# A decode attention and gated MLP kernel: gate scaling folded into the PSUM accumulation, the last V group loaded in quarters, and the small edits beside them

## The chip, the cores and the metric

The kernel runs on one core of a Trainium2 chip. The metric is the device time of one execution in microseconds (us). In the profiles PE is the matmul engine, PEld its weight loads, DVE, ACT and POOL the other compute engines, and SP the engine that issues the loads; the granted clock is the share of its full clock that PE was given. A load has landed when its last byte is in place. Ratios compare runs taken in the same rounds on the same chip.

## The reference

```python
x = A_x                                   # [1, 1, 448], bfloat16
g = sigmoid((x * gate_w).sum(-1))
a = attention(x, k_cache, v_cache, wq, wo) # 16 query heads, 8 KV heads,
                                          # 65536 keys of 256, softmax, then @ wo
gate, up = x @ W_gate, x @ W_up           # [448, 1792]
b = (relu(gate) * up) @ W_down            # [1792, 448]
return g * a + (1 - g) * b
```

The K and V caches are 537 MB. Everything else is small: wq and wo 3.67 MB each, the three MLP ("FFN") weights 1.6 MB each.

## The kernel before

A planner in Python simulates the engines, decides the order of all instructions, and emits them with semaphore waits. All loads are issued in order by one queue (SP). K comes in groups of 4096 rows (2 MB) into a ring of five slots: three for groups that PE transposes and multiplies ("T"), two for groups that DVE reduces ("D"). V comes in groups of 2 MB into a ring of three slots. After the last K group, the FFN weights are loaded over the K ring, while V of the last two heads still has to come.

The parts, with cuts marked by `...`:

```python
# a weight load; extra_w are the K ring slots that the FFN weights overwrite
def emit_wdma(key, dst, src, extra_w=()):
    ...
    return A("sp", lambda e: e.dma_start(dst, src), w=[key] + list(extra_w), dma=(s_w[i], 16), ...)

# rows of a [448, n] weight: 3 x 128 on 128 partitions, then 64 on 64 partitions
def wparts(name, dst, src):
    parts = [(name + "a", dst[:, 0:KFULL, :], src[0:KFULL * 128, :].rearrange("(k p) n -> p k n", p=128))]
    if KREM:
        parts.append((name + "b", dst[0:KREM, KFULL, :], src[KFULL * 128:D, :]))
    return parts

# P @ V: two V rows side by side, so a head's result lies on 4 partitions as two halves
def emit_pv(g, grp, slot, j0, j1, first, last): ...   # 16 matmuls of 128x4 by 128x512 a group

# after the last V group of a head: copy, transpose, scale by 1/denominator, multiply by wo
def emit_oc(g): ...   # ACT copy O_ps -> o_raw, 4x512 float32
def emit_ft(g): ...   # 4 transposes
def emit_on(g): ...   # 4 scalings (half x head)
def emit_am(g): ...   # 8 matmuls into A_ps (half x chunk x head)

def emit_final():
    # DVE: res = b * (1 - g);  res_bf = A_ps * g + res;  then SP stores
    ...
```

In the planner's bookkeeping `w` is a write that must wait for the last writer and all readers of a key. `w2` is a write by one of several writers, which need not wait for each other. A DMA that is the last writer of a key is waited for until it has landed.

## Time and profile before

| | before |
|---|---|
| median of 16 runs (lowest, highest) | 1373.2 us (1371.2, 1379.2) |
| span of the profiled run | 1369.5 us |
| read from HBM | 549.03 MB |
| busy share: PE, DVE, ACT, DMA queue | 82%, 80%, 30%, 96.5% |

The DMA rate of the page, in 40 slices of 34 us. It stays between 381 and 430 GB/s in most slices, and the DMA queue is busy for 96.5% of the span: the loads bound this kernel. Slice 35 (1164 to 1198 us) drops to 273.

```profile
GB/s 341 398 396 423 428 392 416 414 401 404 419 412 425 406 419 396 395 430 416 426 357 421 413 414 429 381 430 398 424 407 362 428 423 411 273 404 428 428 428 260
```

The last 140 us before the last landing carry nothing but V and run at 428 GB/s, one group of 2 MB in 4.90 us. No stretch of 100 us in this trace is above 430 (the highest is 429). I take 428 as an estimate of the full rate, from these 140 us. On that estimate time can only come from stretches in which the DMA engines move less.

What SP waited for (total us, times, longest us). The first three lines are the ring: a load waits for its slot. These waits come to 1196.5 us, and yet the DMA queue was busy for 96.5% of the span, so most of them cost nothing. The last two are different: one FFN weight load waits until the one before it has landed.

```profile
SPq L137 <- PE O_ps L575: 524.0, 93, 17.1
SPq L137 <- PE KTp L430: 419.2, 59, 31.5
SPq L137 <- DVE S_T L460: 253.3, 35, 20.3
...
SPq L363 <- DMA kring<-in_B_W_gate_dram: 17.0, 2, 14.4
SPq L363 <- DMA kring<-in_B_W_up_dram: 9.0, 2, 6.5
```

The same stretch by windows of 10 us. The columns after the length are busy us of PE, PE weight load, DVE, ACT and POOL with their instructions, then granted clock, DMA share and GB/s. Two windows move 110 and 160 GB/s at a DMA share of 0.34 and 0.47.

```profile
1170.00:1180.00 10.00, 6.83 (x31) 2.59 (x32) 6.39 (x36) 0.20 (x1) 0.37 (x1) 1.00 0.99 420
1180.00:1190.00 10.00, 8.39 (x65) 4.25 (x63) 0.33 (x2) 5.94 (x18) 0.46 (x1) 1.00 0.34 110
1190.00:1200.00 10.00, 3.89 (x57) 3.45 (x55) 0.00 (x0) 0.00 (x0) 0.00 (x0) 0.53 0.47 160
1200.00:1210.00 10.00, 2.33 (x33) 2.04 (x32) 0.41 (x3) 0.00 (x0) 0.00 (x0) 0.50 1.06 409
1210.00:1220.00 10.00, 9.70 (x45) 3.74 (x46) 1.06 (x2) 0.00 (x0) 0.00 (x0) 0.78 1.00 428
```

The end (timeline: start, duration, engine, line, operation). The last V group has landed at 1358.6; 10.8 us follow in which no load moves data.

```profile
1358.64 3.62 PE L575 MATMUL O_ps<-vraw,PTd 128*4 128x512 bf16 x16 [1.23 <-DMA vraw<-in_A_v_cache_dram]
1362.30 0.58 ACT L582 COPY o_raw<-O_ps 4x512 f32<-4x512 f32 x1 [77.09 <-PE O_ps L575]
...
1362.93 0.41 PE L590 MATMUL M_ps<-identf,o_raw 4*128 4x4 f32 x4 [0.67 <-ACT o_raw L582]
1363.42 0.72 ACT L602 ACTIVATE oT<-M_ps,rden 128x2 bf16<-128x2 f32 x4 [0.55 <-PE M_ps L590]
...
1364.29 2.84 PE L617 MATMUL A_ps<-wo_sb,oT 128*1 128x448 bf16 x8 [0.95 <-ACT oT L602]
...
1367.25 0.67 DVE L652 SCALAR_TENSOR_TENSOR res_bf<-A_ps,gsc,junk 1x448 bf16<-1x448 f32 x1 [148.38 <-PE A_ps L617]
1367.95 0.31 SPq L655 DMA_DIRECT2D out_dram<-res_bf  x1
```

### The profile page before, as it was taken

What the parts mean: (1) busy time and instruction counts of PE and PEld (TensorE: products, weight loads), DVE (VectorE), ACT (ScalarE), POOL (GpSimd) and SP (SyncE); (2) the same over time, 40 slices, a digit from 0 to 9 for tenths busy, and PEclk for the clock granted to TensorE, in tenths of its full rate; (3) what the DMA queues carried; (4) which work ended last, traced back from release to release, by engine and by line L of the source; (5) the groups of instructions that cost most, each with busy time, mean ns of one, the idle gap of its engine ahead of it and who ended that gap; (6) DMA issues with size and microseconds to landing.
All of it is one profiled execution on the core that took longest, in us unless ns stands there. A gap on an engine that the chain in (4) does not pass through costs nothing.

```text
span 1369.5 us, 20913 instructions
## 1 busy us (share of the span) xinstructions
PE 1117.2 (82%) x6256; PEld 614.2 (45%) x6338; DVE 1094.9 (80%) x6218; ACT 410.3 (30%) x818; POOL 13.7 (1%) x29
## 2 busy tenths in 40 slices
PE   4899899987999669987699966999659896667777
PEld 3577657542664226642265422764227542232222
DVE  1999989999989999899999699989997999300000
ACT  2466556421552105530054400552007420100000
POOL 1000000000000000000000000000000000000000
PEclk9999999998999899998999999999989999879999
DMA  8999999999999999999989999999999999699996
GB/s 341 398 396 423 428 392 416 414 401 404 419 412 425 406 419 396 395 430 416 426 357 421 413 414 429 381 430 398 424 407 362 428 423 411 273 404 428 428 428 260
DMA packets 45300, 550.38 MB, mean 402 GB/s; under 512 B 5185, under 2 KB 11074, under 8 KB 11970
## 3 DMA queue, kind: packets, MB, share of 16 engines
q1 hardware_dynamic: 45186, 549.05, 96.5%
q8 instruction: 49, 0.80, 0.2%
q14 instruction: 65, 0.53, 0.1%
HBM read 549.03 MB, written 0.00 MB: 401 GB/s over the span
## 4 chain that ended last, share of the span: by engine, by line
PE 40%; DMA 38%; DVE 19%; issue 1%; ACT 1%; SPq 1%; ACTq 0%; DVEq 0%
DMA vraw<-in_A_v_cache_dram 23%; DVE junk L460 18%; PE KTp L430 14%; PE S_ps L444 13%; PE O_ps L575 12%; DMA kring<-in_A_k_cache_dram 11%; DMA kring<-in_B_W_gate_dram 1%; DMA vraw<-in_A_wq_dram 1%; DMA kring<-in_B_W_up_dram 1%; PE M_ps L387 1%; DVE MXW L474 1%; DVE S_T L460 1%; SPq L371 0%; ACT kts L435 0%; ACT P_sb L505 0%
## 5 line engine op out<-in xcount | busy, mean ns | idle before, releaser
L460 DVE CUSTOM_DVE_ANT_0 junk<-kring,qb 128x256 bf16<-128x256 bf16 x3072 | 1064.8, 419 | 0.6 <-ACT qb L424 0.2
L435 ACT COPY kts<-KTp 128x512 f32<-128x512 f32 x640 | 347.8, 592 | 382.1 <-PE KTp L430 381.6
L575 PE MATMUL O_ps<-vraw,PT_sb 128*4 128x512 bf16 x1280 | 308.6, 397 | 102.3 <-DMA vraw<-in_A_v_cache_dram 102.1
L430 PE MATMUL KTp<-identf,kring 128*128 128x128 f32 x2560 | 345.2, 277 | 32.2 <-DMA kring<-in_A_k_cache_dram 32.2
L430 PEld LDWEIGHTS KTp<-identf,kring 128*128 128x128 f32 x2560 | 305.3, 143 | 115.2 <-DMA kring<-in_A_k_cache_dram 37.9
L444 PE MATMUL S_ps<-kts,zq 128*128 128x512 bf16 x1198 | 336.8, 390 | 9.4 <-issue 2.6
L575 PE MATMUL O_ps<-vraw,PTd 128*4 128x512 bf16 x768 | 191.4, 407 | 72.7 <-DMA vraw<-in_A_v_cache_dram 72.5
L460 DVE DVE_READ_ACCUMULATOR2_ANT S_T<- 128x1 f32 x3072 | 247.6, 81 | 0.0
L575 PEld LDWEIGHTS O_ps<-vraw,PT_sb 128*4 128x4 bf16 x1280 | 109.2, 90 | 292.9 <-DMA vraw<-in_A_v_cache_dram 129.2
L444 PEld LDWEIGHTS S_ps<-kts,zq 128*128 128x128 bf16 x1280 | 109.6, 98 | 97.3 <-ACT kts L435 40.4
L575 PEld LDWEIGHTS O_ps<-vraw,PTd 128*4 128x4 bf16 x768 | 65.0, 89 | 195.6 <-DMA vraw<-in_A_v_cache_dram 91.2
L582 ACT COPY o_raw<-O_ps 4x512 f32<-4x512 f32 x8 | 4.6, 575 | 413.7 <-PE O_ps L575 413.7
L652 DVE SCALAR_TENSOR_TENSOR res_bf<-A_ps,gsc,junk 1x448 bf16<-1x448 f32 x1 | 0.7, 672 | 148.4 <-PE A_ps L617 148.4
L474 DVE TENSOR_REDUCE MXW<-S_sb 64x1 f32<-64x512 f32 (+1 forms) x32 | 21.7, 678 | 45.8 <-ACT S_sb L450 45.1
L498 ACT ACTIVATE nbias<-negm 128x2 f32<-128x2 f32 x8 | 1.7, 209 | 103.8 <-DVE negm L496 103.8
L387 PE MATMUL M_ps<-xT,vraw 128*128 128x1 bf16 (+1 forms) x128 | 9.2, 174 | 17.4 <-DMA vraw<-in_A_wq_dram 17.4
L505 ACT ACTIVATE P_sb<-S_sb,nbias 64x512 bf16<-64x512 f32 (+1 forms) x32 | 22.9, 717 | 0.6
L402 DVE CAST zq<-M_ps 128x32 bf16<-128x32 f32 x1 | 0.3, 295 | 26.9 <-PE M_ps L394 26.9
L387 PEld LDWEIGHTS M_ps<-xT,vraw 128*128 128x128 bf16 (+1 forms) x128 | 8.3, 106 | 18.2 <-issue 17.3
L617 PE MATMUL A_ps<-wo_sb,oT 128*1 128x448 bf16 x64 | 14.6, 374 | 1.2 <-ACT oT L602 1.2
L545 DVE TENSOR_REDUCE den<-den 128x2 f32<-128x6 f32 x8 | 1.3, 158 | 17.8 <-POOL den L538 17.7
L450 ACT COPY S_sb<-S_ps 128x512 f32<-128x512 f32 x16 | 9.4, 588 | 16.4 <-PE S_ps L444 16.4
(47 smaller groups left out, 103.7 us busy)
## 6 DMA issues: line engine op xcount, KB each, us to landing
kring<-in_A_k_cache_dram SPq DMA_DIRECT2D x128, 2048.0 KB, 12.4
vraw<-in_A_v_cache_dram SPq DMA_DIRECT2D x128, 2048.0 KB, 14.7
wo_sb<-in_A_wo_dram SPq DMA_DIRECT2D x1, 3584.0 KB, 46.1
vraw<-in_A_wq_dram SPq DMA_DIRECT2D x1, 3072.0 KB, 12.1
kring<-in_B_W_down_dram SPq DMA_DIRECT2D x1, 1568.0 KB, 7.2
kring<-in_B_W_gate_dram SPq DMA_DIRECT2D x1, 1344.0 KB, 14.8
kring<-in_B_W_up_dram SPq DMA_DIRECT2D x1, 1344.0 KB, 6.9
vraw<-in_A_wq_dram SPq DMA_DIRECT2D x1, 512.0 KB, 13.6
```

The source lines that it names most:

```text
L387: A("pe", (lambda hc=hc, kt=kt, kk=kk, wv=wv: lambda e: e.matmul(M_ps[:, MC_Q + hc:MC_Q + hc + 1], lhsT=wv, rhs=xT[0:kk, kt:kt + 1], start ...
L430: A("pe", (lambda j=j, jj=jj: lambda e: e.transpose(out=KTp[bank][:, jj * 128:(jj + 1) * 128], in_=tring[:, slot, j, :].bitcast(F32), iden ...
L435: A("act", lambda e: e.copy(out=kts[:, kbuf, :].bitcast(F32), in_=KTp[bank][:, :]), pr=PQ(B_K + bank), w=[("kts", kbuf)], tag=f"ev b{bank} ...
L444: A("pe", (lambda r=r, par=par, rhs=rhs, first=first, last=last: lambda e: e.matmul(S_ps[sphys][:, :], lhsT=zq[:, g, par, 63 - r:191 - r], ...
L450: A("act", lambda e: e.copy(out=S_sb[:, pb, b, :], in_=S_ps[sphys][:, :]), pr=PQ(B_S + sphys), w=[("ssb", pb, b)], tag=f"scopy g{g} b{b}")
L460: A("dve", (lambda j=j, hh=hh, col=col, ji=ji: lambda e: e.tensor_tensor_reduce(out=junk[:, ji, :], in0=dring[:, slot, j, :], in1=qb[:, g, ...
L474: A("dve", (lambda hh=hh, p0=p0: lambda e: e.tensor_reduce(out=MXW[p0:p0 + ns, pb, 2 + 2 * b + hh:3 + 2 * b + hh], in_=S_sb[p0:p0 + ns, pb ...
L498: A("act", lambda e: e.activation(out=nbias[:, pb, :], in_=negm[:, pb, :], func=ACT.Copy, scale=SCALE), r=[("negm", pb)], w=[("nbias", pb) ...
L505: A("act", lambda e: e.activation(out=P_sb[p0:p0 + ns, pb, b, :], in_=S_sb[p0:p0 + ns, pb, b, :], func=ACT.Exp, bias=nbias[p0:p0 + ns, pb, ...
L575: A("pe", (lambda lhs=lhs, rhs=rhs, f_=f_, l_=l_: lambda e: e.matmul(O_ps[qd:qd + 4, 0:2 * DH], lhsT=lhs, rhs=rhs, start=f_, stop=l_))(), ...
L582: A("act", lambda e: e.copy(out=o_raw[qd:qd + 4, :], in_=O_ps[qd:qd + 4, 0:2 * DH]), pr=PQ(B_O, qd, qd + 4), w=[("oraw", pb)], tag=f"oc g{g}")
L617: A("pe", (lambda oc_=oc_, hc=hc, first=first, last=last: lambda e: e.matmul(A_ps[0:1, 0:D], lhsT=oT[:, pb, oc_:oc_ + 1], rhs=wo_sb[:, hc, :],
```

## The change

Its intent, by its title: fold the gate (g and 1 - g) into the accumulation of the output in PSUM, so that the DVE combination at the end goes away, and load the last V group in four parts, so that PE can begin before all of it has landed. The diff holds four more edits that the title does not name. Cut to its core:

```diff
 # 1. claims of the FFN loads
-    return A("sp", ..., w=[key] + list(extra_w), dma=(s_w[i], 16), ...)
+    return A("sp", ..., w=[key], w2=list(extra_w), dma=(s_w[i], 16), ...)
 # 2. start: wq is issued before the tiny x and gate_w loads
-        push_w(small, 4096)
-        push_w(wparts("wq", wq_sb, A_wq), ..., done=wq_done)
+        push_w(wparts("wq", wq_sb, A_wq), ...)
+        push_w(small, 4096, done=wq_done)
 # 3. gate: [g, 1-g] broadcast once by POOL; g into the scaling of a head's result ...
+            A("pool", lambda e: e.partition_all_reduce(gb[:], gz[:], 128, ...add), ...)
+            A("dve", ... rdg[:, g, :] = rden[:, g, :] * gb[:, 0:1])
 #    ... and 1-g into h; the down-projection accumulates into A_ps as well
-                    O_ps[64:65, 0:D], lhsT=hT[:, ft:ft + 1], rhs=wd_sb[:, ft, :], ...
+                    A_ps[0:1, 0:D], lhsT=hT[:, ft:ft + 1], rhs=wd_sb[:, ft, :], start=False, stop=False))(),
-            # DVE: b * (1-g), then A_ps * g + that; SP stores
+            A("act", lambda e: e.activation(out=res_bf[:], in_=A_ps[0:1, 0:D], func=ACT.Copy), ...)  # ACT stores
 # 4. the two halves of a head's result are summed while transposing: 4 float32 matmuls with a
 #    selection matrix instead of 4 transposes; 2 scalings instead of 4; 4 wo matmuls instead of 8
+                        M_ps[:, col:col + 2], lhsT=o_raw[qd:qd + 4, part * DH + c * 128:...],
+                        rhs=identf[qd:qd + 4, qd + 2 * part:...], start=(part == 0), stop=(part == 1)
 # 5. every V group is handed to PE in four quarters (planner), score matmuls may come between
+                    for part in range(VSUB):
+                        arrived[c].append((g, grp, slot, part))
 # 6. the last V group of the last head is also loaded in four quarters
+            split = (c == "V" and g == HKV - 1 and grp == NG - 1)
```

The instruction streams, compared engine by engine, show that the order of the loads is otherwise the same. The waits on the weight loads' semaphores are gone.

More of the change, by code (lines that the diff above doesn't have):

```diff
@@ L208, in bass_gated_mix__gqa_block_cached__glu_gated_reglu__decode_kernel @@
     F = B_W_gate.shape[1]
-    assert DH == 256 and HQ == 2 * HKV and F % 128 == 0
+    assert DH == 256 and HQ == 2 * HKV and F % 128 == 0 and HKV >= 2
     NC2 = 2
@@ L296, in bass_gated_mix__gqa_block_cached__glu_gated_reglu__decode_kernel @@
         hT = sb("hT", [128, FT], BF16)
-        b_sb = sb("b_sb", [1, D], F32)
         gsc = sb("gsc", [1, 4], F32)
@@ L308, in bass_gated_mix__gqa_block_cached__glu_gated_reglu__decode_kernel @@
         o_raw = sb("o_raw", [64, 2 * DH], F32)
-        oT = sb("oT", [128, 2, 8], BF16)
-        res = junk[0:1, :, :].rearrange("p a d -> p (a d)").bitcast(F32)[:, 0:D]
+        oT = sb("oT", [128, 2, 4], BF16)
+        gz = sb("gz", [128, 2], F32)
+        gb = sb("gb", [128, 2], F32)
+        rdg = sb("rdg", [128, HKV, 2], F32)
         res_bf = sb("res_bf", [1, D], BF16)
@@ L352, in emit_consts @@
             A("pool", lambda e: e.memset(warm[:], 0.0), w=["warm"])
+            A("pool", lambda e: e.memset(gz[:], 0.0), w=["gzz", "gz0"])
             A("pool", lambda e: e.partition_all_reduce(warm[:, 2:4], warm[:, 0:2], 128, bass.bass_isa.ReduceOp.max),
@@ L362, in emit_wdma, with emit_group_dma @@
             wsem_i[0] += 1
-            return A("sp", lambda e: e.dma_start(dst, src), w=[key] + list(extra_w), dma=(s_w[i], 16), tag=f"wdma {key}")
-        def emit_group_dma(cls, g, grp, slot):
+            return A("sp", lambda e: e.dma_start(dst, src), w=[key], w2=list(extra_w), dma=(s_w[i], 16), tag=f"wdma {key}")
+        VSUB = 4 if J % 8 == 0 else 2
+        JP = J // VSUB
+        s_vsub = [sem(f"s_vsub{i}") for i in range(VSUB)]
+        vsub_cnt = [0] * VSUB
+        def emit_group_dma(cls, g, grp, slot, part=None):
             src_t = A_v_cache if cls == "V" else A_k_cache
@@ L369, in emit_group_dma @@
             dst = ring[:, slot, :, :]
-            ring_cnt[cls][slot] += 1
-            A("sp", lambda e: e.dma_start(dst, src), w=[(cls, slot)],
-              after=(wq_readers if cls == "V" and ring_cnt[cls][slot] == 1 else ()),
-              dma=(ring_sems[cls][slot], 16 * ring_cnt[cls][slot]), tag=f"dma{cls} g{g} grp{grp}")
+            if part is None:
+                ring_cnt[cls][slot] += 1
+                first_use = ring_cnt[cls][slot] == 1
+                keys = [(cls, slot)] if cls != "V" else [("V", slot, p_) for p_ in range(VSUB)]
+                dsem = (ring_sems[cls][slot], 16 * ring_cnt[cls][slot])
+            else:
+                src = src[:, part * JP:(part + 1) * JP, :]
+                dst = dst[:, part * JP:(part + 1) * JP, :]
+                vsub_cnt[part] += 1
+                first_use = False
+                keys = [("V", slot, part)]
+                dsem = (s_vsub[part], 16 * vsub_cnt[part])
+            A("sp", lambda e: e.dma_start(dst, src), w=keys,
+              after=(wq_readers if cls == "V" and first_use else ()),
+              dma=dsem, tag=f"dma{cls} g{g} grp{grp}")
         x_keys = ["xT0"] + (["xT1"] if KREM else [])
@@ L409, in emit_zq @@
               r=[("gsc", 0), ("gsc", 2)], w=[("gsc", 3)])
+            A("dve", lambda e: e.tensor_copy(out=gz[0:1, :], in_=gsc[0:1, 2:4]), r=[("gsc", 2), ("gsc", 3)], w=["gz0"], tag="gz")
+            A("pool", lambda e: e.partition_all_reduce(gb[:], gz[:], 128, bass.bass_isa.ReduceOp.add),
+              r=["gz0", "gzz"], w=["gb"], tag="gb")
         def emit_qb_mm(g, bank):
@@ L548, in emit_rcp @@
               tag=f"rcp g{g}")
+            A("dve", lambda e: e.tensor_scalar(out=rdg[:, g, :], in0=rden[:, g, :], scalar1=gb[:, 0:1], scalar2=None,
+                                               op0=AluOpType.mult), r=[("rden", g), "gb"], w=[("rdg", g)], tag=f"rdg g{g}")
         def slot_of(g, ti, j):
@@ L576, in emit_pv @@
                     O_ps[qd:qd + 4, 0:2 * DH], lhsT=lhs, rhs=rhs, start=f_, stop=l_))(),
-                  r=[("V", slot)] + rk, pw=PQ(B_O, qd, qd + 4), tag=f"pv g{g} grp{grp}")
+                  r=[("V", slot, j // JP)] + rk, pw=PQ(B_O, qd, qd + 4), tag=f"pv g{g} grp{grp}")
         def emit_oc(g):
@@ L587, in emit_ft @@
             qd = 32 * pb
-            for i in range(4):
-                col = MC_OT + pb * 16 + i * 4
-                A("pe", (lambda i=i, col=col: lambda e: e.transpose(
-                    out=M_ps[:, col:col + 4], in_=o_raw[qd:qd + 4, i * 128:(i + 1) * 128],
-                    identity=identf[qd:qd + 4, qd:qd + 4]))(),
-                  r=[("oraw", pb), "identf"], pw=PQ(B_M), tag=f"ft g{g}")
+            for c in range(NC2):
+                col = MC_OT + pb * 4 + c * 2
+                for part in range(2):
+                    A("pe", (lambda c=c, col=col, part=part: lambda e: e.matmul(
+                        M_ps[:, col:col + 2], lhsT=o_raw[qd:qd + 4, part * DH + c * 128:part * DH + (c + 1) * 128],
+                        rhs=identf[qd:qd + 4, qd + 2 * part:qd + 2 * part + 2], start=(part == 0), stop=(part == 1)))(),
+                      r=[("oraw", pb), "identf"], pw=PQ(B_M), tag=f"ft g{g}")
         def emit_on(g):
             pb = g % 2
-            for part in range(2):
-                for hh in range(2):
-                    c0 = MC_OT + pb * 16 + part * 8 + 2 * part + hh
-                    src = M_ps[:, c0:c0 + 8].rearrange("p (c k) -> p c k", k=4)[:, :, 0]
-                    dst = oT[:, pb, part * 4:part * 4 + 4].rearrange("p (c h) -> p h c", h=2)[:, hh, :]
-                    A("act", (lambda src=src, dst=dst, hh=hh: lambda e: e.activation(
-                        out=dst, in_=src, func=ACT.Copy, scale=rden[:, g, hh:hh + 1]))(),
-                      r=[("rden", g)], pr=PQ(B_M), w=[("oT", pb, part, hh)], tag=f"on g{g}")
+            for hh in range(2):
+                src = M_ps[:, MC_OT + pb * 4:MC_OT + pb * 4 + 4].rearrange("p (c h) -> p h c", h=2)[:, hh, :]
+                dst = oT[:, pb, :].rearrange("p (c h) -> p h c", h=2)[:, hh, :]
+                A("act", (lambda src=src, dst=dst, hh=hh: lambda e: e.activation(
+                    out=dst, in_=src, func=ACT.Copy, scale=rdg[:, g, hh:hh + 1]))(),
+                  r=[("rdg", g)], pr=PQ(B_M), w=[("oT", pb, hh)], tag=f"on g{g}")
         def emit_am(g):
@@ L608, in emit_am @@
             n = 0
-            for part in range(2):
-                for c in range(NC2):
-                    for hh in range(2):
-                        n += 1
-                        first = (g == 0 and n == 1)
-                        last = (g == HKV - 1 and n == 4 * NC2)
-                        hc = (2 * g + hh) * NC2 + c
-                        oc_ = part * 4 + c * 2 + hh
-                        A("pe", (lambda oc_=oc_, hc=hc, first=first, last=last: lambda e: e.matmul(
-                            A_ps[0:1, 0:D], lhsT=oT[:, pb, oc_:oc_ + 1], rhs=wo_sb[:, hc, :],
-                            start=first, stop=last))(),
-                          r=[("oT", pb, a_, b_) for a_ in range(2) for b_ in range(2)] + ["wo"], pw=PQ(B_A, 0, 1),
-                          tag=f"am g{g}")
+            for c in range(NC2):
+                for hh in range(2):
+                    n += 1
+                    first = (g == 0 and n == 1)
+                    last = (g == HKV - 1 and n == 2 * NC2)
+                    hc = (2 * g + hh) * NC2 + c
+                    A("pe", (lambda c=c, hh=hh, hc=hc, first=first, last=last: lambda e: e.matmul(
+                        A_ps[0:1, 0:D], lhsT=oT[:, pb, 2 * c + hh:2 * c + hh + 1], rhs=wo_sb[:, hc, :],
+                        start=first, stop=last))(),
+                      r=[("oT", pb, 0), ("oT", pb, 1), "wo"], pw=PQ(B_A, 0, 1), tag=f"am g{g}")
         def emit_gu(which):
@@ L636, in emit_h @@
             A("dve", lambda e: e.tensor_copy(out=u_bf[:], in_=M_ps[:, MC_U:MC_U + FT]), pr=PQ(B_M), w=["u_bf"], tag="h")
-            A("dve", lambda e: e.tensor_tensor(out=hT[:], in0=g_bf[:], in1=u_bf[:], op=AluOpType.mult),
-              r=["g_bf", "u_bf"], w=["hT"], tag="h")
+            A("dve", lambda e: e.scalar_tensor_tensor(out=hT[:], in0=g_bf[:], scalar=gb[:, 1:2], in1=u_bf[:],
+                                                      op0=AluOpType.mult, op1=AluOpType.mult),
+              r=["g_bf", "u_bf", "gb"], w=["hT"], tag="h")
         def emit_bm():
@@ L642, in emit_bm @@
                 A("pe", (lambda ft=ft: lambda e: e.matmul(
-                    O_ps[64:65, 0:D], lhsT=hT[:, ft:ft + 1], rhs=wd_sb[:, ft, :], start=(ft == 0), stop=(ft == FT - 1)))(),
-                  r=["hT", "wd"], pw=PQ(B_O, 64, 65), tag="bmm")
-        def emit_bcopy():
-            A("dve", lambda e: e.tensor_copy(out=b_sb[:], in_=O_ps[64:65, 0:D]), pr=PQ(B_O, 64, 65), w=["b_sb"], tag="bcopy")
+                    A_ps[0:1, 0:D], lhsT=hT[:, ft:ft + 1], rhs=wd_sb[:, ft, :], start=False, stop=False))(),
+                  r=["hT", "wd"], pw=PQ(B_A, 0, 1), tag="bmm")
         def emit_final():
-            A("dve", lambda e: e.tensor_scalar(out=res[:], in0=b_sb[:], scalar1=gsc[0:1, 3:4], scalar2=None, op0=AluOpType.mult),
-              r=[("gsc", 3), "b_sb"], w=["res"] + [("junk", i) for i in range(4)], tag="fin0")
-            A("dve", lambda e: e.scalar_tensor_tensor(out=res_bf[:], in0=A_ps[0:1, 0:D], scalar=gsc[0:1, 2:3], in1=res[:],
-                                                      op0=AluOpType.mult, op1=AluOpType.add),
-              r=[("gsc", 2), "res"], pr=PQ(B_A, 0, 1), w=["res_bf"], tag="fin1")
-            od = A("sp", lambda e: e.dma_start(out[0, :, :], res_bf[:]), r=["res_bf"], dma=(s_out, 16), tag="out")
-            A("sp", None, after=[od], tag="final wait")
+            A("act", lambda e: e.activation(out=res_bf[:], in_=A_ps[0:1, 0:D], func=ACT.Copy),
+              pr=PQ(B_A, 0, 1), w=["res_bf"], tag="fin")
+            od = A("act", lambda e: e.dma_start(out[0, :, :], res_bf[:]), r=["res_bf"], dma=(s_out, 16), tag="out")
+            A("act", None, after=[od], tag="final wait")
         MB = 1.0 / 0.428e6
@@ L662, in bass_gated_mix__gqa_block_cached__glu_gated_reglu__decode_kernel @@
         D_V = (J // 2) * 0.225
+        D_VP = D_V / VSUB
         D_DSUB = 8 * 0.348
@@ L712, in pe_work_ahead @@
             w += sum(NBLK * (D_TP + D_QK) for _ in arrived["T"])
-            w += sum(D_V for _ in arrived["V"])
+            w += sum(D_VP for _ in arrived["V"])
             return w
@@ L761, in pick_dma, with start0 @@
             pri, c, g, grp, slot = cands[0]
+            split = (c == "V" and g == HKV - 1 and grp == NG - 1)
+            if split:
+                def start0():
+                    ring_free[c][slot] = False
+                    ring_fill[c] = (slot + 1) % ring_n[c]
+                    issued[c] += 1
+                    emit_group_dma(c, g, grp, slot, part=0)
+                for part in range(1, VSUB):
+                    dma_q.insert(part - 1, (T_DMA_GRP / VSUB + 0.15,
+                                            (lambda part=part: lambda: emit_group_dma(c, g, grp, slot, part=part))(),
+                                            (lambda part=part: lambda: arrived[c].append((g, grp, slot, part)))(),
+                                            lambda: True))
+                return (T_DMA_GRP / VSUB + 0.15, start0, lambda: arrived[c].append((g, grp, slot, 0)))
             def start():
@@ L772, in done @@
                 inflight[c] -= 1
-                arrived[c].append((g, grp, slot))
+                if c == "V":
+                    for part in range(VSUB):
+                        arrived[c].append((g, grp, slot, part))
+                else:
+                    arrived[c].append((g, grp, slot))
             return (T_DMA_GRP, start, done)
@@ L839, in pick_pe @@
             if arrived["V"]:
-                g, grp, slot = arrived["V"][0]
+                g, grp, slot, part = arrived["V"][0]
                 can_v = chain[g].get("done") and (g < 2 or fin[g - 2].get("oc"))
@@ L878, in pick_pe, with start, done @@
             if choose == "V":
-                g, grp, slot = arrived["V"].pop(0)
-                first = v_done[g] == 0 and not vcur.get(("started", g))
-                vcur[("started", g)] = True
+                g, grp, slot, part = arrived["V"].pop(0)
                 cnt = vcur.get(("cnt", g), 0) + 1
                 vcur[("cnt", g)] = cnt
-                last = cnt == NG
-                def start(g=g, grp=grp, slot=slot, first=first, last=last):
-                    emit_pv(g, grp, slot, 0, J, first, last)
-                def done(g=g, slot=slot, last=last):
-                    ring_free["V"][slot] = True
-                    v_done[g] += 1
+                first = cnt == 1
+                last = cnt == NG * VSUB
+                def start(g=g, grp=grp, slot=slot, part=part, first=first, last=last):
+                    emit_pv(g, grp, slot, part * JP, (part + 1) * JP, first, last)
+                def done(g=g, slot=slot, part=part, last=last):
+                    if part == VSUB - 1:
+                        ring_free["V"][slot] = True
+                        v_done[g] += 1
                     if last:
                         start_fin(g)
-                return (D_V, start, done)
+                return (D_VP, start, done)
             if misc.get("ffn_q"):
@@ L1030, in am_done, with queue_am @@
                             if g == HKV - 1:
-                                misc["am_last"] = True
-                                try_final()
-                        pe_q.append((1.6, lambda: emit_am(g), am_done))
+                                act_q.append((0.3, emit_final, lambda: misc.__setitem__("all_done", True)))
+                        def queue_am():
+                            if g < HKV - 1 or misc.get("b_done"):
+                                pe_q.append((0.8, lambda: emit_am(g), am_done))
+                            else:
+                                S.at(S.now + 0.2, queue_am)
+                        queue_am()
                     def queue_on():
                         if chain[g].get("rden"):
-                            act_q.append((0.9, lambda: emit_on(g), on_done))
+                            act_q.append((0.5, lambda: emit_on(g), on_done))
                         else:
@@ L1042, in start_fin @@
             act_q.append((0.3, lambda: emit_oc(g), oc_done))
-        def try_final():
-            if misc.get("am_last") and misc.get("b_done") and not misc.get("final"):
-                misc["final"] = True
-                dve_q.append((0.4, emit_final, lambda: misc.__setitem__("all_done", True)))
         def done_all():
@@ L1108, in pump_qb @@
                 S.at(S.now + 0.3, pump_qb)
-        push_w(wparts("wq", wq_sb, A_wq), D * HQ * DH * 2, done=wq_done)
+        push_w(wparts("wq", wq_sb, A_wq), D * HQ * DH * 2)
+        push_w(small, 4096, done=wq_done)
         misc["started"] = False
@@ L1127, in h_done, with queue_bm @@
                 def h_done():
-                    def bm_done():
-                        dve_q.append((0.3, emit_bcopy, lambda: (misc.__setitem__("b_done", True), try_final())))
-                    pe_q.append((FT * 0.2, emit_bm, bm_done))
+                    def queue_bm():
+                        if fin[0].get("am"):
+                            pe_q.append((FT * 0.2, emit_bm, lambda: misc.__setitem__("b_done", True)))
+                        else:
+                            S.at(S.now + 0.2, queue_bm)
+                    queue_bm()
                 dve_q.append((0.5, emit_h, h_done))
```

## The prediction

> **What bounds the kernel now.** It streams 549 MB from HBM, and the DMA queue sets the time. In the windows view, most 20 us windows move 415 to 430 GB/s, and in the last 140 us (V of the last head only) each V group of 2 MB lands 4.90 us after the one before (428 GB/s) while its 16 matmuls take 3.62 us. [...] 549 MB at 428 GB/s is 1283 us; the span is 1369.5. The other 87 us are the start (about 4 us before data flows), an end of 13 us without data, one gap at 1180 to 1202 us, and some 50 us in many bubbles of 0.5 to 4 us in the body, when the in-order SP queue waits for PE or DVE to free a ring slot.
>
> **The gap.** From 1180 to 1202 us the windows show 184, 5, 87, 317, 61 and 181 GB/s: some 14 us of transfer time lost. The waits view of SP says why: 26 us of waits of one FFN weight load for the one before it (17.0 on W_gate, 9.0 on W_up). The old code claims the ring slots again in every load, so each waits for its predecessor's landing, and V loads behind them are held too. In the changed program the waits on the weight semaphores are gone; order of issue is the same. This is in the diff as a small thing (the extra keys become a multi-writer claim), but it is the largest gain. I keep 1.5 us of it as lost: V restarts with the down-projection matmuls between the first V matmuls, at a low granted clock. Gain 12.5 us.
>
> **The end.** Chain in the timeline after the last V landing (1358.6): 16 matmuls 3.62, copy 0.58, transposes 0.41, four scalings 0.72, eight matmuls 2.84, DVE combination 0.67, output DMA. After: the last group comes in four quarters, so only 4 matmuls (about 1.0) follow the last landing (-2.6); two scalings (-0.35); four output matmuls (-1.4); an ACT copy for the DVE step (-0.1); the float32 selection matmuls may cost +0.3. Gain 4.2 us, all critical.
>
> **The start.** Wq is issued 2.3 us earlier (before: 3.05 us), the tiny x and gate loads after it. [...] PE starts at about 16 instead of 17.37 us. Gain 1.5 us.
>
> **Off the path.** The extra DVE, POOL and gate broadcast operations (under 1 us each), and the matmuls saved in heads 0 to 6 (0.8 us each, hidden under DMA). V matmuls in quarters let score matmuls in between; the bubbles of the body move by perhaps 3 us either way.
>
> **Sum.** 12.5 + 4.2 + 1.5 = 18 us of 1373.6: predicted 1355 us, 8 in 10 between 1347 and 1364. Faster by over 2% (under 1346): 0.08; within 2%: 0.91; slower: 0.01.
>
> **Right or wrong would show as:** SP waits on W_gate and W_up near zero; windows around 1180 to 1202 at or above 400 GB/s; last V landing to the end of the span about 7 us instead of 10.9; PE's first matmul near 16 us; DMA mean about 407 GB/s.
>
> **What would make it wrong:** V waits for its slot after the FFN loads because PE is held by matmuls waiting for weights, which moves the gap instead of filling it; quarters of 4 KB rows transfer slower; x behind wq lands late and delays all; or the finer PE order opens or closes bubbles in the body by more than 5 us.

12.5 + 4.2 + 1.5 come to 18.2 us, rounded to 18. The start gains 1.5 us and not the whole 2.3 by which wq is issued earlier; that was my estimate, from the 2.3 us. The 1.5 us kept for the restart of V and the +0.3 for the selection matmuls, which the kernel before doesn't have, were guesses with no measured number behind them.

## The result, and the profile after

| | before | after |
|---|---|---|
| median (lowest, highest) | 1373.2 us (1371.2, 1379.2), 16 runs | 1363.7 us (1360.4, 1366.7), 11 runs |
| span of the profiled run | 1369.5 us | 1363.2 us |
| end after the last V landing | 10.8 us | 8.2 us |

The ratio is 0.9927, 95% interval 0.9913 to 0.9940. Ratios here are the mean time of one kernel's runs over that of the other's runs in the same rounds, so not quite the ratio of the medians. The gain is 10 us or 0.7%, inside the stated range of 1347 to 1364 us, but by 0.3 us: 5 of the 11 runs lie above 1364, so that the median fell inside is partly luck. 10 us came of the 18 that the sum promised.

SP no longer waits for weights:

```profile
SPq L137 <- PE O_ps L598: 516.2, 180, 16.5
SPq L137 <- PE KTp L451: 410.6, 60, 25.5
SPq L137 <- DVE S_T L481: 262.6, 36, 20.0
```

But the windows that held the gap did not rise to 400 GB/s. They show 323 and 336 GB/s at a DMA share of 0.99 and 1.11: the engines are busy and move too little. A second, smaller hole, 326 GB/s at a share of 0.86, is at 1210 to 1220 us, where there was none:

```profile
1180.00:1190.00 10.00, 8.78 (x48) 3.87 (x46) 0.71 (x4) 5.92 (x17) 0.83 (x2) 1.00 0.99 323
1190.00:1200.00 10.00, 7.95 (x112) 7.08 (x112) 0.00 (x0) 0.00 (x0) 0.00 (x0) 0.59 1.11 336
1200.00:1210.00 10.00, 5.03 (x17) 1.76 (x17) 0.48 (x3) 0.00 (x0) 0.00 (x0) 0.56 1.00 426
1210.00:1220.00 10.00, 10.00 (x48) 3.88 (x45) 0.00 (x0) 0.00 (x0) 0.00 (x0) 1.00 0.86 326
```

The end. The last quarter landed at 1355.0, yet PE is busy until 1357.0. It works without a pause from 1349.96, because it got the group before the last as a whole and was still on it when the first quarters came:

```profile
1349.96 3.62 PE L598 MATMUL O_ps<-vraw,PT_sb 128*4 128x512 bf16 x16 [1.29 <-DMA vraw<-in_A_v_cache_dram]
...
1353.41 3.62 PE L598 MATMUL O_ps<-vraw,PTd 128*4 128x512 bf16 x16
1357.07 0.58 ACT L605 COPY o_raw<-O_ps 4x512 f32<-4x512 f32 x1 [75.34 <-PE O_ps L598]
...
1357.70 1.05 PE L614 MATMUL M_ps<-identf,o_raw 4*128 4x2 f32 x8 [0.67 <-ACT o_raw L605]
1358.83 0.42 ACT L624 ACTIVATE oT<-M_ps,rdg 128x2 bf16<-128x2 f32 x2 [1.19 <-PE M_ps L614]
...
1359.40 1.65 PE L637 MATMUL A_ps<-wo_sb,oT 128*1 128x448 bf16 x4 [0.65 <-ACT oT L624]
...
1361.08 0.53 ACT L667 ACTIVATE res_bf<-A_ps 1x448 bf16<-1x448 f32 x1 [1.83 <-PE A_ps L637]
1361.64 0.50 ACTq L669 DMA_DIRECT2D out_dram<-res_bf  x1
```

The output matmuls (L617 before, L637 after) depend on the granted clock of the moment, the third number from the right. Windows around them, first before (eight matmuls, clock 0.57), then after (four, clock 0.50):

```profile
1364.20:1367.20 3.00, 2.84 (x8) 0.84 (x8) 0.00 (x0) 0.00 (x0) 0.00 (x0) 0.57 0.00 0
```

```profile
1359.30:1361.10 1.80, 1.65 (x4) 0.36 (x4) 0.00 (x0) 0.02 (x1) 0.00 (x0) 0.50 0.00 0
```

In the other kernels the same four took 0.92 us at a clock of 1.00 (e2, e9), 0.94 at 0.89 (e3) and 1.56 at 0.54 (e5), and the eight 1.96 at 0.82 (e1). So up to 0.7 us of an end is a matter of which clock the run had there.

To see where transfer time is lost, the DMA packets of each trace were summed by stage: lost time = length of the stage minus its bytes at 428 GB/s. The "FFN stage" runs from 3 us before the last K landing to 25 us after the last FFN weight landing; "body" lies between 40 us and that stage; "end" is the time after the last V landing. All are us of one profiled run each. The packets' clock was aligned so that the landing of a V group meets the start of the matmuls that waited for it, which is good to about 0.1 us. What is lost between the FFN stage and the last landing, 1.1 to 2.0 us and in two runs (three groups split, padded combination) 2.9 and 3.2 us, is left out.

```
                    start(0-40)   body   FFN stage   end
before                  7.7      48.0     15.1      10.8
after                   6.0      53.3      7.7       8.2
claims alone            7.9      52.6      7.9       9.9
V groups whole          5.9      49.0      5.9       7.4
three groups split      6.0      52.6      8.4       6.4
long rows               6.0      51.2      7.5       8.2
old claims back         5.9      50.8     16.4       8.1
down-proj. later        5.9      54.2      6.9       8.1
112-row tiles           9.6      52.7     12.9       7.4
fold alone              7.9      51.0     15.8       9.0
padded row tile         6.0      51.8      4.9       7.5
combination, padded     6.1      56.6      3.6       5.6
combination             6.1      50.2      7.2       5.6
```

In this pair of profiles the FFN stage gave 7.4 us, the end 2.6 and the start 1.7, and the body took 5.3 back. The experiments asked whether the body's loss is real, why the FFN stage gave 7.4 and not 12.5, and why the end gave 2.6 and not 4.2.

### The profile page after: what moved, and what is told of

The parts are those of the page before. It is cut to its first block, busy times and chain, and to the rows that moved or that the text cites. A ratio compares the mean times of both kernels' runs of the same rounds, so it can differ in the third digit from the quotient of the medians.

```text
span 1363.2 us, 21006 instructions
## 1 busy us (share of the span) xinstructions
PE 1126.2 (83%) x6257; PEld 617.8 (45%) x6338; DVE 1095.3 (80%) x6224; ACT 408.6 (30%) x803; POOL 14.4 (1%) x31
## 4 chain that ended last, share of the span: by engine, by line
PE 47%; DMA 32%; DVE 19%; issue 1%; ACT 1%; SPq 1%; ACTq 0%
DMA vraw<-in_A_v_cache_dram 21%; DVE junk L481 17%; PE KTp L451 16%; PE S_ps L465 16%; PE O_ps L598 13%; DMA kring<-in_A_k_cache_dram 10%; DMA xT<-in_A_x_dram 1%; PE M_ps L405 1%; DVE MXW L495 0%; DVE S_T L481 0%; SPq L389 0%; ACT P_sb L526 0%; PE A_ps L662 0%; ACT kts L456 0%; ACT S_sb L471 0%
## 5 line engine op out<-in xcount | busy, mean ns | idle before, releaser
L598 PE MATMUL O_ps<-vraw,PT_sb 128*4 128x512 bf16 x1280 | 314.3, 401 | 92.0 <-DMA vraw<-in_A_v_cache_dram 92.0
L481 DVE DVE_READ_ACCUMULATOR2_ANT S_T<- 128x1 f32 x3072 | 252.7, 82 | 0.0
L510 POOL PARTITION_ALL_REDUCE mall<-MXW x8 | 3.6, 449 | 1043.7 <-DVE MXW L504 1043.7
L614 PE MATMUL M_ps<-identf,o_raw 4*128 4x2 f32 x64 | 8.4, 249 | 5.3 <-ACT o_raw L605 5.3
## 6 DMA issues: line engine op xcount, KB each, us to landing
vraw<-in_A_v_cache_dram SPq DMA_DIRECT2D x127, 2048.0 KB, 13.9
```

The lines of the kernel that those rows point to most:

```text
L481: A("dve", (lambda j=j, hh=hh, col=col, ji=ji: lambda e: e.tensor_tensor_reduce(out=junk[:, ji, :], in0=dring[:, slot, j, :], in1=qb[:, g, ...
L510: A("pool", lambda e: e.partition_all_reduce(mall[:, pb, 0:nc6], MXW[:, pb, 0:nc6], 128, bass.bass_isa.ReduceOp.max), r=[("MXW", pb, c) fo ...
L598: A("pe", (lambda lhs=lhs, rhs=rhs, f_=f_, l_=l_: lambda e: e.matmul(O_ps[qd:qd + 4, 0:2 * DH], lhsT=lhs, rhs=rhs, start=f_, stop=l_))(), ...
L614: A("pe", (lambda c=c, col=col, part=part: lambda e: e.matmul(M_ps[:, col:col + 2], lhsT=o_raw[qd:qd + 4, part * DH + c * 128:part * DH + ...
```

## The experiments

Each was timed in five rounds against the kernel before (four to six runs of each, beside eleven of the kernel before). The change itself was timed in rounds of its own, so a variant is compared with it only through the kernel before. The edits shown are cut to their core. Eleven kernels ran, and all gave the reference's result within its tolerance. One variant was not run: loading the 64-row parts of W_gate and W_up at the start, into a tile of their own; what it would have given is not shown.

| run | median us | ratio to before | 95% interval |
|---|---|---|---|
| the change | 1363.7 | 0.9927 | 0.9913 to 0.9940 |
| e1_claims | 1367.5 | 0.9947 | 0.9928 to 0.9965 |
| e2_whole_v | 1362.0 | 0.9911 | 0.9894 to 0.9928 |
| e3_split3 | 1363.7 | 0.9924 | 0.9905 to 0.9943 |
| e4_long_rows | 1363.2 | 0.9920 | 0.9904 to 0.9936 |
| e5_old_claims | 1371.8 | 0.9985 | 0.9963 to 1.0008 |
| e6_late_bm | 1362.2 | 0.9903 | 0.9883 to 0.9923 |
| e8_k112 | 1373.1 | 0.9992 | 0.9974 to 1.0010 |
| e9_fold_only | 1374.1 | 0.9994 | 0.9976 to 1.0012 |
| e10_pad | 1360.9 | 0.9905 | 0.9887 to 0.9923 |
| e11_best | 1358.2 | 0.9896 | 0.9872 to 0.9920 |
| e12_combo | 1358.8 | 0.9890 | 0.9872 to 0.9908 |

### e1_claims: one line of the change alone

```diff
 # on the kernel before
-    return A("sp", ..., w=[key] + list(extra_w), dma=(s_w[i], 16), ...)
+    return A("sp", ..., w=[key], w2=list(extra_w), dma=(s_w[i], 16), ...)
```

> The kernel before with one line of the change alone: the FFN weight loads claim the ring slots as multi-writer claims, so they no longer wait for one another. Theory A (the prediction): the gap at 1180 to 1202 us is pure waiting and nearly all of it (12.5 us of 14) comes back, time about 1361 us, ratio 0.991. Theory B (from the profile after the change): about 7 us come back, because the weights themselves move at only 320 to 340 GB/s and V restarts late; time about 1366 us, ratio 0.995. In both the SP waits on W_gate and W_up are zero and the end after the last V landing stays 10.9 us.

Measured: ratio 0.9947, which is 7.3 us (interval 4.8 to 9.9), and 15.1 us lost in the FFN stage became 7.9. Theory B holds: 12.5 us lies outside the interval. The step is most of the change's gain, but worth little more than half of what was forecast. The end was 9.9 us, not 10.8: the eight output matmuls took 1.96 us here against 2.84, with the same instructions but a granted clock of 0.82 against 0.57. The body lost 52.6 us although its instructions are in the order of the kernel before (48.0).

### e5_old_claims: everything but that line

```diff
 # on the changed kernel
-    return A("sp", ..., w=[key], w2=list(extra_w), dma=(s_w[i], 16), ...)
+    return A("sp", ..., w=[key] + list(extra_w), dma=(s_w[i], 16), ...)
```

> The changed kernel with the old claims put back, so the FFN weight loads wait for one another again and everything else of the change stays. If the parts add up (claims worth about 7 us, the end 2.6, the start 1.5), this is 3 to 5 us faster than before: about 1370 us, ratio 0.997. Rival: the rest of the change is worth nothing, ratio 1.000; or the prediction's claims worth 12.5 us were right and the rest loses: ratio above 1.002. SP waits of some 26 us on W_gate and W_up are back.

Measured: ratio 0.9985, and SP waits on W_gate and W_up again:

```profile
SPq L365 <- DMA kring<-in_B_W_gate_dram: 17.0, 2, 14.3
SPq L365 <- DMA kring<-in_B_W_up_dram: 9.4, 2, 6.7
```

Against the change's 0.9927 the line is worth 0.0058 of 1374, or 8.0 us (by both intervals some 4 to 12); from the other side it was 7.3. Within this noise the parts add up. The rest of the change is worth some 2 us, with an interval that reaches zero.

### e9_fold_only: the titled first half

```diff
 # on the changed kernel: old claims, old start order, and
-                    for part in range(VSUB):
-                        arrived[c].append((g, grp, slot, part))
+                    arrived[c].append((g, grp, slot, "all"))
-            split = (c == "V" and g == HKV - 1 and grp == NG - 1)
+            split = False
```

> The change's titled first half alone: gate scaling folded into PSUM accumulation (and the two halves summed by the selection matmuls), with the old claims, the old start order, and V groups whole and unsplit. From the changed profile's end: selection matmuls +0.65, scalings -0.30, output matmuls -1.2, last step -0.14, so the end after the last V landing is 9.9 us in place of 10.9 and the time falls by 1.0 us, too little for the interval (ratio 0.998 to 1.001). Rival: the fold also takes load off the body and is worth 3 us or more.

Measured: 0.9994, not to be told from nothing. The end after the last landing was 9.0 us. It is better than the 9.9 expected because the four output matmuls took 0.92 us here, at a granted clock of 1.00, and 1.65 in the change's profile, at 0.50, again with the same instructions. So the fold saves 1 to 2 us at the end and nothing that can be measured elsewhere.

### e2_whole_v: is the body's loss real?

```diff
 # on the changed kernel
-                    for part in range(VSUB):
-                        arrived[c].append((g, grp, slot, part))
+                    arrived[c].append((g, grp, slot, "all"))     # 16 matmuls at once, as before
```

> The changed kernel, but V groups are handed to PE whole, as before; only the last group is still taken in quarters. Theory A (finer PE order opened bubbles in the body): 3 to 5 us faster than the changed kernel, about 1359 us. Theory B (the body's loss in the one profile is variation from run to run): within 1.5 us of 1363.7. Either way the V restart after the FFN loads should lose less than the 2.2 us seen at 1212 to 1217 us, since the down-projection matmuls then stand behind the first V group and not inside it.

Measured: median 1362.0 against 1363.7, intervals overlapping. The body lost 49.0 us in this profile. Read alone, that would look like the 4 us of theory A. But the kernels with V groups whole lost 48.0, 52.6, 49.0, 51.0, 50.2 and 56.6 us in the body (before, e1, e2, e9, e12, e11), and those with quarters 50.8 to 54.2. The spread within one kind is larger than the difference. The body's 5.3 us in the first pair of profiles are mostly variation from run to run; that the finer order costs 1 or 2 us is possible and stays open. The hole at the restart of V shrank as expected: 1.3 us were lost in the 20 us from the first V matmul, 2.3 in the change.

### e3_split3: why the split gave less

```diff
-            split = (c == "V" and g == HKV - 1 and grp == NG - 1)
+            split = (c == "V" and g == HKV - 1 and grp >= NG - 3)   # own semaphores for each group
```

> The changed kernel with the last three V groups of the last head in quarters in place of the last one. Theory A: the split is worth less than forecast because PE gets the group before the last whole, is busy with it 3.62 us and so is behind when the quarters land; then PV work after the last landing falls from 2.07 us to about 1.0 us and the time by about 1.1 us. Theory B: quarters move more slowly than whole groups; then the last landing comes later and nothing is gained.

Measured: PE now takes each quarter as it lands and is idle before it. 1.0 us of PV follows the last landing, not 2.07, and the end fell from 8.2 to 6.4 us. Of these 1.8 us the split gave 1.0; 0.7 came from the output matmuls, which had a clock of 0.89 here and 0.50 in the change:

```profile
1352.17 1.02 PE L597 MATMUL O_ps<-vraw,PTd 128*4 128x512 bf16 x4 [0.25 <-DMA vraw<-in_A_v_cache_dram]
1353.45 1.02 PE L597 MATMUL O_ps<-vraw,PTd 128*4 128x512 bf16 x4 [0.25 <-DMA vraw<-in_A_v_cache_dram]
1354.69 1.02 PE L597 MATMUL O_ps<-vraw,PTd 128*4 128x512 bf16 x4 [0.21 <-DMA vraw<-in_A_v_cache_dram]
1355.93 1.02 PE L597 MATMUL O_ps<-vraw,PTd 128*4 128x512 bf16 x4 [0.21 <-DMA vraw<-in_A_v_cache_dram]
```

So the backlog is shown. Theory B has a part in it too: quarters came every 1.24 to 1.28 us, four of them in 4.96 to 5.12 us against 4.90 for a whole group, the stretch before the last landing lost 2.9 us where the change lost 1.9, and the time did not move (1363.7). A gain of 1 us is below what these runs can tell.

### e4_long_rows: are short runs in HBM the cause of the low rate?

```diff
-src[0:KFULL * 128, :].rearrange("(k p) n -> p k n", p=128)      # also x and gate_w
+src[0:KFULL * 128, :].rearrange("(p k) n -> p k n", p=128)
-B_W_down.rearrange("(f p) n -> p f n", p=128)
+B_W_down.rearrange("(p f) n -> p f n", p=128)
-lhsT=w_sb[0:kk, kt, ft * 128:(ft + 1) * 128]
+lhsT=w_sb[0:kk, kt, :].rearrange("p (n f) -> p f n", f=FT)[:, ft, :]
```

> The changed kernel with x, gate vector, wq and the three FFN weights loaded so that each partition's rows lie together in HBM (10.7 KB, 24 KB and 12.5 KB runs in place of 3.6 KB, 8 KB and 0.9 KB), the matmuls' columns permuted to match. Theory A: in the changed kernel the FFN weights move at 320 to 340 GB/s because of their short runs; with long ones 1180 to 1200 us shows 410 GB/s or more and the time falls by 3 to 5 us. Theory B: what is left of the gap comes from waiting; the rate and the time stay.

Measured: no gain beyond noise (1363.2), FFN stage 7.5 against 7.7. From 1180 to 1190 us the rate was 327 GB/s, much as before the edit (323); from 1190 to 1200 it rose to 390. So run length explains little of it. The 112 gate and up matmuls, whose weights are now read with a stride of 14 columns, took 11.83 us instead of 8; whether that cost some of it again is not shown. The packets themselves told more. Alone, a packet of 10,752 bytes took 404 ns; where the load of the 64 remaining rows was in flight, its neighbours took 487 to 703 ns in the mean of 2 us each. In the change's own trace, 3584-byte packets took 141 to 145 ns in the mean of 2 us each until 1186 us, and 153 to 308 ns from there to 1196 us, with packets of both row counts in these means.

### e8_k112: no 64-row loads, but no 128-row loads either

```diff
-    KT = (D + 127) // 128;  KFULL = D // 128;  KREM = D - KFULL * 128
+    KP = 112;  KT = KFULL = D // KP;  KREM = 0        # 448 = 4 x 112
```

> The changed kernel with the 448 rows of x, wq, W_gate and W_up cut as 4 x 112 rather than 3 x 128 + 64, so that the loads on 64 partitions are gone (run lengths stay 3.6 and 8 KB). Theory A: the 64-row loads, whose packets already took 196 ns against 144 ns when alone in the kernel before, slow the loads they now overlap (packets of 167 to 281 ns); without them the weights move at 144 to 160 ns a packet, 1180 to 1195 us shows 390 GB/s or more and 2 to 3 us come back, and about 1 us at the start, where wq's 64-row part took 528 ns a packet against 309. Theory B: overlap of any kind is what slows them; packets stay above 170 ns and the time stays.

Measured: both theories fell. The kernel lost nearly all the change's gain (1373.1), because these loads are slow by themselves. At the start, with nothing but wq in flight, most of its 8 KB packets took some 510 to 630 ns (means of 1 us) where 128-row loads take 309; the third quarter of them was faster, 393 ns in the mean. The windows 4 to 8 us, first of the change and then of this run:

```profile
4.00:8.00 4.00, 0.00 (x0) 0.00 (x0) 0.00 (x0) 0.00 (x0) 1.31 (x1) 1.00 1.01 422
```

```profile
4.00:8.00 4.00, 0.00 (x0) 0.00 (x0) 0.00 (x0) 0.00 (x0) 1.32 (x1) 1.00 1.03 240
```

Both have a DMA share above 1; one moves 422 GB/s and the other 240, with packets of the same 8 KB. What differs is how the load lies on the partitions: 112 rows at a time here, 128 in the change. Loads on 64 rows are not all alike. The last 64 packets of wq, its 64-row part, took 539 ns in the mean of the change's trace against 309 (the record's 528 is a slightly different count). For W_gate it is not as plain: alone in the kernel before, 45 of the 64 packets of its 64-row part took 138 to 140 ns, no more than those on 128 partitions (140), and the other 19 up to 594. Why loads on 112 or 64 partitions are slower, no run here shows.

One thing got faster: the 128 wq matmuls took 3.55 us with 112 rows each, instead of 9.22 with three tiles of 128 rows and one of 64 in turn. What costs the time in the mixed order, no run here shows.

### e10_pad: only loads on 128 partitions

```diff
 # last row tile: rows 320..447 on 128 partitions, x zero in the doubled rows
-    ksz = [128] * KFULL + ([KREM] if KREM else [])
+    ksz = [128] * KT
+            A("pool", lambda e: e.memset(xT[:], 0.0), w=["xT0", "xT1"])
-                parts.append((name + "b", dst[0:KREM, KFULL, :], src[KFULL * 128:D, :]))
+                parts.append((name + "b", dst[:, KFULL, :], src[D - 128:D, :]))
```

> The changed kernel with the last row tile of x, gate vector, wq, W_gate and W_up loaded as rows 320 to 447 on 128 partitions, x being zero in the doubled rows; no load of weights covers 64 partitions any more, at the price of 0.98 MB more, about 2.3 us. The run with 112 rows showed that loads not covering all 128 partitions move at half rate by themselves (wq packets of 8 KB 533 to 565 ns against 309). Theory A: the 64-row loads are what slows the FFN weights in the changed kernel; now the 3.6 KB packets take 140 to 160 ns throughout and the rate at 1184 to 1192 us rises above 390 GB/s, and the net gain is 0 to 2 us because of the added bytes. Theory B: overlapping loads slow each other anyhow; packets stay at 170 to 280 ns and the time rises by about 2 us. Beside it: with one shape of matmul the gate and up matmuls should take about 30 ns each instead of 71, as they did with 112 rows.

What the record says of "loads not covering all 128 partitions" is wider than the number beside it, which was measured on wq with 112 partitions.

Measured: theory A. With the loads overlapping as in the change, 3584-byte packets took 141 to 150 ns throughout, and the two windows that showed 323 and 336 GB/s show:

```profile
1180.00:1190.00 10.00, 9.01 (x54) 4.06 (x53) 0.70 (x4) 5.92 (x17) 0.46 (x1) 1.00 1.00 403
1190.00:1200.00 10.00, 3.00 (x112) 2.85 (x110) 0.48 (x3) 0.00 (x0) 0.00 (x0) 0.71 1.06 413
```

The shorter gate and up matmuls (3.1 us in place of 8.0) are no rival for this: PE stood idle for 7.3 us after them, waiting for V. The FFN stage lost 4.9 us against 7.7 (in the combination, e11 and e12 below, 3.6 against 7.2), at a price of 0.98 MB more (2.3 us at 428 GB/s, half of it here and half at the start). The median is 1360.9, 2.9 us under the change; the intervals overlap (0.9887 to 0.9923 against 0.9913 to 0.9940). That the 64-row loads slowed the others is shown, the net gain is likely and not settled. The wq matmuls, of one shape now, first in the change and then here:

```profile
15.33 9.22 PE L405 MATMUL M_ps<-xT,vraw 128*128 128x1 bf16 x128 [15.33 <-DMA xT<-in_A_x_dram]
```

```profile
16.82 3.56 PE L406 MATMUL M_ps<-xT,vraw 128*128 128x1 bf16 x128 [16.82 <-DMA xT<-in_A_x_dram]
```

### e6_late_bm: the hole at 1210 to 1220 us

```diff
-                        if fin[0].get("am"):
+                        if fin[0].get("am") and v_done[HKV - 2] >= NG // 2:   # down-projection later
```

> The changed kernel with the 14 down-projection matmuls moved from inside the first V group after the FFN loads to eight V groups later. Theory: they hold that V group, hence its slot, for some 3.9 us at a low granted clock, and this makes the 2.2 us hole at 1212 to 1217 us; with them later the hole shrinks to under 1 us and 1210 to 1220 us shows over 390 GB/s instead of 326; time about 1 to 2 us less. Rival: the low clock alone makes the hole; it stays.

Measured: the window went from 326 to 351 GB/s, not over 390, and the stage from 7.7 to 6.9 us. The time, 1362.2, is not told apart from the change's. Without the 14 matmuls in it, the first V group was done in 6.09 us, where it held its slot for 8.2 us in the change; 3.62 is usual. The granted clock was 0.50 until 1212.0:

```profile
1200.00:1210.00 10.00, 5.35 (x41) 2.97 (x41) 0.48 (x3) 0.00 (x0) 0.00 (x0) 0.50 1.02 435
1210.00:1220.00 10.00, 9.77 (x41) 3.51 (x40) 0.00 (x0) 0.00 (x0) 0.00 (x0) 0.90 0.88 351
```

The clock came back to 1.00 5.05 us after the first V matmul here, 3.9 us in the change. PE's wait of 4.65 us for V did not bring it down: it stood at 0.50 since 1195.0, while the gate and up matmuls still ran. What sets it, no run here shows.

So the theory fell in size, and the hole is not the clock's alone either. In the 20 us from the first V matmul, kernels with the down-projection inside the first V group lost 2.3 (the change), 4.1 (e3), 3.2 (e4), 2.7 (e8) and 3.2 us (e10), and those with it later 1.8 (e6), 0.8 (e11) and 1.2 (e12). The half clock lasted 3.3 to 6.0 us into V in the first and 4.3 to 5.8 in the others, so it doesn't sort them. e11 and e12 also have V groups whole; how the hole is shared between clock, order and matmuls is not settled.

### e11_best and e12_combo: the parts together

The edits of e2, e6, a split of the last two groups as in e3, and o_raw in bfloat16, so that the selection matmuls are bfloat16 as well: e12. With the padded row tile of e10 as well: e11.

> Combination: the changed kernel with V groups whole, the last two groups in quarters, down-projection later, o_raw in bfloat16 [...], and the padded row tile. Expected from the parts: end after the last V landing about 6.0 us instead of 8.2, FFN stage 2 us better, whole groups 0 to 2 us: about 1359 us. Rival: the parts drown in the variation of the body and it is within 1.5 us of the changed kernel.

> The same combination without the padded row tile. Expected about 1360 us; the difference from the padded one is what the padding is worth here (0 to 2 us if the first theory of the padded run holds, minus 2 us if not).

Measured: 1358.2 and 1358.8 us. Both medians lie under the change's. For e12 the intervals just fail to overlap (0.9872 to 0.9908 against 0.9913 to 0.9940); e11 has runs from 1355.9 to 1365.1, two of them near 1365, and its interval overlaps the change's. Its profile fell on the slowest of these runs, and there the body lost 56.6 us. The end was 5.6 us in both, about as expected, with the selection matmuls of a head at 0.25 us (4 records) instead of 1.05 (8 records); the output matmuls took 0.92 us, as in e2 and e9. Whether padding helps within the combination is not settled. No version here is 2% faster than before.

## Why the prediction was right or wrong

**Right: the bound, and where the gain would come from.** The SP waits on W_gate and W_up went from 26 us to none, and that one line is worth 7.3 us added alone (e1) or 8.0 taken away (e5), more than all else together. The time lay inside the range.

**Right: the start.** Forecast 1.5 us, PE at about 16 us. PE began at 15.33 instead of 17.37, and the first 40 us lost 6.0 us of transfer instead of 7.7. The loads of x, issued after wq, landed after it, the two parts at 14.1 and 15.2 us against 13.9.

**Wrong in size: "Gain 12.5 us" for the gap.** It was 7 to 8. The term assumed that, once nothing waits, 4.8 MB of weights move at 428 GB/s, and kept 1.5 us for the restart of V. The FFN stage still lost 7.7 us. Three parts of that have a number:

- Loads on 64 partitions slowed those they overlapped: 2.8 us (7.7 to 4.9 in e10). The trace of before had shown a sign at wq, whose last 64 packets took 643 ns in the mean against 309. I had read waits and GB/s by window there and not packet times.
- W_down comes in runs of 896 bytes: 41 ns a packet (21.9 bytes a ns) against 33.4 at the rate of the 16384-byte packets, 611 ns each (26.8 bytes a ns); those of 3584 bytes, where no 64-row load was beside them, took 141 ns (25.4). An estimate from these, over 1792 packets on 16 engines: 0.85 us.
- The restart of V cost 2.3 us (packet sums of the hole at 1212 to 1217 us) and not 1.5. The mechanism had been named: the down-projection inside the first V group, at a low clock (e6).

The remaining 1.8 us are not attributed.

**Wrong in size: "Gain 4.2 us" at the end.** It was 2.6. The term "-2.6" for the split was -1.55: only 4 matmuls wait for the last quarter, but PE is still busy with the whole group before it (3.62 + 3.62 us of work against 4.90 us between landings). e3 removed that backlog. The selection matmuls cost +0.64 and not +0.3: the trace has 64 float32 matmuls for the 32 of the program, 246 ns each against 198 for a transpose. The output matmuls gave -1.2 and not -1.4: half the count, but at a clock of 0.50 against 0.57.

**Not contradicted, though the first pair of profiles seemed to: the body** "moves by perhaps 3 us either way". Of the 5.3 us in that pair, 4.6 also lie between two profiles with one and the same instruction order (before and e1).

In sum: claims 7.3 to 8.0, end 2.6, start 1.7 make 11.6 to 12.3 us; measured were 10.0 us, interval 8.2 to 12.0, so 1 or 2 us may have been lost elsewhere.

## What to carry to other kernels

Look for waits between DMAs that come only from bookkeeping: one line that let five loads be issued together was worth more here than the restructured arithmetic that gave the change its name. But do not price a removed wait at the peak rate until you have read the packet times of those very loads, since busy engines can move little: in e8, with wq on 112 partitions, their share was 1.03 at 240 GB/s, and in the change, on 128, 1.01 at 422. And when a transfer is split so that its consumer starts early, check that the consumer is idle when the first part arrives; if it is behind by one whole piece, as PE was here, the piece before has to be split as well (2.07 us of PV after the last landing, 1.0 in e3).
